# A sliding-window attention block with a gated MLP on one core: the split MLP weights are made once, kept in device memory and loaded as parts

## The chip, the core and the metric

The kernel runs on one core of a Trainium2 chip. The metric is the device time of one execution in microseconds. The kernel before took 1002.38 us as the median of three runs (999.41 to 1004.93).

The engines have these names here and in the profile: PE or TensorE (matrix products; PEld is its loading of weights), DVE or VectorE, ACT or ScalarE, POOL or GpSimd, and SP or SyncE, which in this kernel only issues transfers. Each of them works through its own instructions in program order.

## The reference, cut to what matters

```python
# x: 1 x 2048 x 640; wqkv 640 x 1920; wo 640 x 640; w1 640 x 1536; w2 1536 x 640
sa, ca, ga, sb, cb, gb = split6(silu(c) @ w_mod)          # each of 640
h = layernorm(x) * (1 + ca) + sa
q, k, v = heads(h @ wqkv)                                 # 32 heads of 20
p = softmax(mask(q @ k.T / sqrt(20)))                     # causal, window of 256
x = x + ga * (merge(p @ v) @ wo)
h = layernorm(x) * (1 + cb) + sb
y = layernorm(h)
x = x + gb * (gelu(y @ w1 + b1) @ w2 + b2)
```

All data is float32.

## The kernel before, in words

**Two parts for each operand.** Every large product is made from operands split into a high part (a copy rounded to the type `fp32r`) and a low part (the operand less its high part). Three products of parts, high by high, high by low and low by high, are added up. A split therefore costs a copy for the high part and a subtraction for the low part; the weights `w1` and `w2` are split like the activations.

**The attention** is a loop over steps `t`, some 3.7 us each from t = 12 (102 us) to t = 84 (380 us). A step makes scores for one block of 128 queries and four heads, takes their maximum, exponentiates transposed scores made eleven steps behind (LAG), and multiplies by v. Between these, each step does a number of products for q, k and v (`unit`), whose parts go through device memory (`q_scr`, `k_scr`) before they are loaded again for the scores (`rows_in`, 5 steps or so ahead). Everything else is hung on quarter steps by `spread(plan, steps, lo, hi)`: a list of closures under the key (t, quarter), run in that order. Tables of numbers at the top of the file (EXTRA, EARLY, AFTER, LNS, MODS, WOS, W1S, RS, TAIL_AT and more) say how many products a step takes and when each side task comes. MODS places the sums for three of the modulation vectors (`mod_steps`).

**The row blocks.** The 16 blocks of 128 rows go through the steps of `mid_steps`: load `ob`, scale (`om`), split (`oh`, `ol`), output product `wo`, add to x (`xb`), statistics, modulation and norm (`y`), transposes of x (`xt`) and y (`yt`), split of the transposed y (`yhi`, `ylo`). Four of them run during the last attention steps, the rest between the products of the MLP.

**The MLP** begins at about 576 us. It works through a written list, PLAN: a word is an operation (`ops`), a number says how many TensorE closures (`pe`) come next. Each TensorE closure is three products of 128 x 512. The rows stand in four chunks of 512, taken in pairs; p is the pair. For f = 0 to 5 the products P1 and P2 use a column block of w1 as it is; for i = 0 to 5 the products P3 to P7 use five sums and differences of the column blocks i and i + 6 of w1 (`w1_sums`, tile `cm`, tag `ws`), so that fewer products serve both chunks. `second(j, ms)` multiplies the gelu result j (0 to 47) by a row block of w2 and adds it to the five output sums.

**The weights in the MLP.** Each part is made again for each pair: `w1_load` (L855) and `w2_load` (L860) fetch a raw block of 320 KB on SP; `w1_high`, `w1_low`, `w1_sums`, `ws_high`, `ws_low`, `w2_high` and `w2_low` (L1607 to L1650) make the parts. High parts are copied on ACT; the engine of each low part and sum stands in a string, W1E, SUME, WSE or W2E (d DVE, p POOL). 36 raw blocks of w1 and 48 of w2 are loaded and split in all. GHE and GLE name the engines that split the gelu results (`ghi`, `glo`). The sixth modulation vector, the gate `gb`, is summed in the MLP too (tile `wm5`, words `gl`, `gs`, `gt`, `go`).

Two lines show the form of a split, here of w2:

```python
nc.scalar.copy(tl["w2", j][0], wt["w2", j])
engines[W2E[j]].tensor_tensor(lo, wt["w2", j], f32(hi), ALU.subtract)
```

All instructions carry the line L193, the helper that keeps them in program order, so the profile is read by tile names.

Of the kernel before, what the change touches and what calls it, by code (L numbers as in the profile page):

```python
# [9 lines left out]
F32 = mybir.dt.float32  # L10
# [31 lines left out]
UNITS = ((0, 'q1', 'k1', 'v0', 'v1', 'k2', 'q2', 'v2', 'q3', 'k3', 'v30', 'k40', 'q40', 'v40', 'q41', 'k41', 'v31', 'v41'), (1, 'k00', 'q10', 'q00', 'k10', 'q01', 'k01', 'k11', 'q11', 'v0', 'v1', 'k2', 'q2', 'q3', 'k3', 'v2', 'q4', 'v3', 'k4', 'v4'))  # L42
FAST = 10
LNS = [-9.75, -3.75, -1.0, -1.5, 0.75, -0.75, 0.0]
LOV = [1, 2, 3, 7, 8, 17, 18, 23, 24, 25, 35, 36, 37, 41, 43, 47, 52, 55, 57, 58]
HIA = [0, 4, 7]
# [10 lines left out]
EXTRA = {9: -2, 10: -3, 11: 5, 14: -4, 15: 3, 16: -4, 17: 2, 18: 1, 19: -3, 20: -4, 21: 6, 22: 1, 23: 1, 25: 4, 26: -3, 27: 3, 28: -3, 29: 7, 30: -5, 31: 1, 32: -3, 33: -1, 34: -1, 35: -3, 36: 3, 37: 9, 38: -8, 39: 3, 40: -3, 41: -8, 42: -2, 43: 3, 44: -3, 45: 9, 46: 3, 47: -1, 48: 4, 50: 1, 51: -3, 52: -16, 53: 7, 54: -5, 55: 4, 56: -7, 57: 13, 58: -1, 59: 10, 60: -1, 61: 3, 63: 2, 64: -1, 65: 10, 66: -4, 67: -1, 69: 2, 70: -4, 71: 4, 72: 3, 73: 3, 75: -9, 76: -2, 77: -3, 78: -1, 79: -1, 80: -4, 81: -9, 82: 15, 83: 6, 84: -2, 85: 2, 86: 2, 87: 11, 88: 4, 89: -9, 90: 3, 91: 1, 92: 3, 93: -6, 94: -12, 95: 1, 96: 1, 98: 3, 99: 2, 100: 2, 101: 7, 102: -3, 103: 6, 104: -4, 105: -1, 106: -6, 107: -2, 108: -1, 109: 7, 110: 1, 111: 3, 112: 4, 114: -1}  # L57

EARLY = {1: (4, 0, 0), 2: (5, 0, 0), 3: (5, 0, 0), 4: (2, 0, 0), 5: (3, 0, 0), 7: (3, 0, 0), 9: (5, 0, 0), 10: (5, 0, 0), 12: (1, 0, 0), 13: (0, 0, 0), 14: (0, 0, 0), 15: (5, 0, 0), 16: (5, 0, 0), 17: (4, 0, 0), 19: (4, 0, 0), 20: (2, 0, 0), 21: (4, 0, 0), 23: (5, 0, 0), 24: (1, 0, 0), 25: (1, 0, 0), 30: (5, 0, 0), 32: (0, 0, 0), 33: (3, 0, 0), 35: (5, 0, 0), 36: (1, 0, 0), 37: (5, 0, 0), 42: (1, 0, 0), 43: (2, 0, 0), 44: (5, 0, 0), 45: (5, 0, 0), 49: (4, 0, 0), 50: (3, 0, 0)}

AFTER = {0: 1, 2: 1, 4: 3, 5: 1, 6: 1, 7: 1, 8: 1, 9: 1, 10: 2, 11: 1, 12: 2, 14: 1, 15: 2, 19: 1, 20: 1, 21: 1, 22: 1, 23: 2, 25: 1, 27: 1, 32: 1, 34: 1, 35: 1, 36: 1, 38: 1, 39: 1, 40: 3, 41: 1, 43: 2}

SUMS_LAST = [14, 15, 18, 23, 25, 26, 27, 29, 35, 42, 50, 57, 59, 63, 64, 74, 76, 79, 83, 86, 88, 91, 92, 95, 101, 105, 106, 110, 116, 117, 118, 120, 121, 122, 123, 126, 129, 132, 133, 135, 136, 139]
LEAST = 4
CUT = 3
WHOLE = [11, 12, 23, 24, 26, 28, 29, 31, 38, 39, 40, 42, 43, 44, 45, 47, 50, 53, 55, 57, 60, 63, 75, 76, 84, 86, 90, 108, 109, 111, 112, 115, 116, 121, 122, 124, 125, 126, 127]
MOST = 10
MODS = [[8.75, 17.0], [18.75, 27.0], [70.25, 79.0]]
WOS = [89.25, 94.0, 99.0, 109.0, 111.75, 114.25, 115.75]
W1S = [118.25, 123.5, 135.0]  # L70
RS = [[79.5, 82.5], [86.0, 87.0]]
TOMID = 109
WARM = {(115, 0): 1, (121, 0): 3, (127, 2): 1, (130, 1): 2, (135, 0): 4, (136, 0): 10, (114, 3): 6, (120, 3): 1, (135, 2): 1}
LATE_AT = [105.75, 106.5, 106.75, 108.75, 110.25, 111, 113.25]
TAIL0 = [115.25, 120.25, 124.25, 129.25]
NEXT = [133.869, 138.565]
CROSS = [1.165, -0.035]
# [121 lines left out]
def block_kernel(ctx: ExitStack, tc: tile.TileContext, x, wqkv, wo, w1, b1, w2, b2, c, crow, wmod, wcol, sel, outT):  # L199
# [665 lines left out]
    def w1_steps():  # L865

        def load():
            w1_load(0)
            w1_load(1)
            w2_load(0)  # L870
# [942 lines left out]
```

## Time and profile before

| | |
|---|---|
| median of three runs | 1002.38 us |
| the profiled execution | 1001.14 us |
| its span, first to last instruction | 999.4 us |
| mean granted TensorE clock | 0.992 |
| attention, row blocks 0 to 4 or so | 0 to about 576 us |
| MLP and the other row blocks | about 576 to 999.4 us |
| moved by DMA | 160.05 MB, mean 160 GB/s |

A row of a stage gives the stretch, then each engine's busy time with its instructions in brackets, the granted share of the TensorE clock, the busy share of 16 DMA engines and the rate. A row of a group names engine, operation, output and inputs (with the buffer numbers left out), shapes, the count, busy time and mean length in ns, and after a bar the idle time of the engine before them with what ended it. A row of waits gives total time, times and the longest.

### The profile page before, as it was taken

The page shows a single profiled execution, that of the slowest core. Times are in us where ns is not written, and L with a number is a line of the kernel's source. Part 1 is how long each engine was busy: PE and PEld are TensorE (multiplying, and loading weights), DVE is VectorE, ACT ScalarE, POOL GpSimd, SP SyncE. Part 2 cuts the span into 40 slices and gives each one's busy share as a digit, 9 for nine tenths or more (in the row PEclk, how much of TensorE's full clock was granted, in tenths as well). Part 3 has the DMA queues.
Part 4 walks back from the last instruction along what each step waited for, and adds up shares of the span by engine and source line. Part 5 has one row for each costly group of instructions (what it writes and reads, how often), then busy time and mean ns, then how long its engine had stood idle before and what let it go on. Part 6 is the DMA issues. An engine that isn't in the chain of part 4 may idle for free.

```text
span 999.4 us, 20268 instructions
## 1 busy us (share of the span) xinstructions
PE 944.9 (95%) x7719; PEld 741.5 (74%) x7719; DVE 723.6 (72%) x1140; ACT 473.7 (47%) x830; POOL 534.0 (53%) x672
## 2 busy tenths in 40 slices
PE   9999999999999999999988988889999989989998
PEld 8777777777777777776776867768887777767876
DVE  6564877888767877777898688794658878766553
ACT  3724555656654555555545553543334435533232
POOL 3423555677873545645445566974334539952142
PEclk8999999999999999999999999999999999999999
DMA  8366778564787569566562274432227533421063
GB/s 302 105 216 189 244 239 269 170 206 148 232 244 192 165 189 279 160 168 190 148 170 75 78 240 129 131 102 72 79 67 235 169 111 117 125 83 53 27 186 104
DMA packets 102433, 160.05 MB, mean 160 GB/s; under 512 B 9248, under 2 KB 42496, under 8 KB 102336
## 3 DMA queue, kind: packets, MB, share of 16 engines
q1 hardware_dynamic: 93120, 150.37, 50.1%
q10 hardware_dynamic: 9216, 8.39, 2.7%
q8 instruction: 61, 1.00, 0.4%
q14 instruction: 36, 0.29, 0.1%
HBM read 106.38 MB, written 51.58 MB: 158 GB/s over the span
## 4 chain that ended last, share of the span: by engine, by line
PE 67%; DVE 18%; ACT 5%; issue 4%; DMA 3%; POOL 2%; SPq 0%; DVEq 0%; ACTq 0%; POOLq 0%
PE pp L193 16%; PE P L193 12%; PE out L193 9%; PE e L193 7%; PE o L193 7%; PE s L193 4%; PE wo L193 4%; ACT pt L193 3%; DVE e L193 3%; PE ppo L193 2%; DVE glo L193 2%; DVE nm L193 1%; DVE cm L193 1%; DMA ob<-o_scr 1%; DVE ghi L193 1%
## 5 line engine op out<-in xcount | busy, mean ns | idle before, releaser
L193 POOL TENSOR_SCALAR_AFFINE_SELECT pt<-pt 128x512 f32<-128x512 f32 x192 | 130.0, 677 | 138.6 <-ACT pt L193 131.5
L193 ACT ACTIVATE pt<-e 128x1024 f32<-128x1024 f32 (+1 forms) x120 | 133.7, 1114 | 65.3 <-DVE e L193 63.1
L193 DVE TENSOR_REDUCE nm<-s 128x1 f32<-128x256 f32 (+4 forms) x206 | 157.6, 797 | 4.4
L193 POOL TENSOR_TENSOR w2lo<-w2r,w2hi 128x640 fp32r<-128x640 f32 x46 | 81.4, 1770 | 96.3 <-ACT w2hi L193 85.7
L193 PE MATMUL e<-qbuf,kbuf 62*128 62x128 f32 (+2 forms) x773 | 111.8, 328 | 10.4 <-ACT pt L193 9.0
L193 PEld LDWEIGHTS e<-qbuf,kbuf 62*128 62x128 f32 x773 | 80.7, 185 | 49.5 <-ACT pt L193 25.6
L193 DVE COPY_PREDICATED e<-mask_t,e 128x512 f32<-128x512 uint32 x96 | 66.6, 694 | 68.8 <-PE e L193 62.5
L193 PE MATMUL pp<-hhi,w_hi 128*128 128x512 f32 x265 | 114.0, 430 | 0.2 <-ACT pf L193 0.2
L193 PE MATMUL s<-kbuf,qbuf 60*128 60x384 f32 (+2 forms) x728 | 105.9, 302 | 4.2 <-DVE nm L193 1.9
L193 PE MATMUL pp<-hlo,w_hi 128*128 128x512 f32 x265 | 108.4, 409 | 0.2 <-POOL hlo L193 0.2
L193 PE MATMUL pp<-hhi,w_lo 128*128 128x512 f32 x265 | 106.3, 401 | 0.0
L193 PE MATMUL out<-glo,w2hi 128*128 128x512 f32 x240 | 94.9, 395 | 7.2 <-DVE glo L193 7.0
L193 PEld LDWEIGHTS s<-kbuf,qbuf 60*128 60x128 f32 x728 | 89.2, 186 | 14.1 <-DVE nm L193 5.8
L193 PE MATMUL o<-pt,vbuf 128*32 128x128 f32 x2688 | 99.5, 277 | 0.0
L193 PE MATMUL out<-ghi,w2hi 128*128 128x512 f32 x240 | 96.5, 402 | 0.4 <-DVE xr L193 0.4
L193 PE MATMUL out<-ghi,w2lo 128*128 128x512 f32 x240 | 94.2, 392 | 0.1
L193 POOL TENSOR_TENSOR w_lo<-wraw,w_hi 128x128 fp32r<-128x128 f32 x171 | 76.0, 476 | 31.6 <-ACT w_hi L193 31.6
L193 ACT COPY oT<-o 128x128 f32<-128x128 f32 x128 | 33.9, 265 | 119.1 <-PE o L193 112.1
L193 DVE COPY_PREDICATED s<-mask_t,s 128x512 f32<-128x512 uint32 x112 | 77.1, 689 | 13.8 <-PE s L193 13.5
L193 PEld LDWEIGHTS o<-pt,vbuf 128*32 128x32 f32 x2688 | 66.9, 109 | 15.0 <-issue 2.7
L193 PEld LDWEIGHTS pp<-hhi,w_hi 128*128 128x128 f32 x265 | 49.9, 188 | 20.4 <-issue 11.3
L193 ACT ACTIVATE gs<-gs,b_sb 128x512 f32<-128x512 f32 x24 | 17.4, 723 | 89.3 <-DVE gs L193 89.3
(445 smaller groups left out, 2155.8 us busy)
## 6 DMA issues: line engine op xcount, KB each, us to landing
w2r<-in_w SPq DMA_DIRECT2D x48, 320.0 KB
qbuf<-q_scr SPq DMA_DIRECT2D x60, 240.0 KB
wraw<-in_wqkv SPq DMA_DIRECT2D x36, 320.0 KB
w1r<-in_w SPq DMA_DIRECT2D x36, 320.0 KB
kbuf<-k_scr SPq DMA_DIRECT2D x44, 240.0 KB
q_scr<-stage SPq DMA_DIRECT2D x20, 512.0 KB
k_scr<-stage SPq DMA_DIRECT2D x20, 512.0 KB
o_scr<-oT ACTq DMA_DIRECT2D x64, 128.0 KB
```

Of the source, the lines that this page charges most:

```text
L193: return self.tc.keep_in_program_order(op(*args, **kw))
```

## The change: weights split once and kept

- The parts of w1 (column blocks 0 to 5), of w2 (twelve row blocks) and of the sums of blocks (six times twelve blocks of 128 x 128) are made once, by `prepare()`, between about t = 8 and t = 86 of the attention, and stored in three new buffers of device memory, `w1_scr`, `w2_scr` and `ws_scr`. A piece is a copy on ACT, a subtraction on the engine in PREPE (31 times POOL, 5 times DVE) a quarter step later, and a store on SP some steps later (PREPS). There are 36 pieces: 18 of 640 columns, and for each of the six sums three of 384, 640 and 512 columns. The five additions of a sum run on the engines in the new SUME (25 times POOL, 5 times DVE). A raw block is loaded AHEAD = 4 steps before its piece.
- In the MLP, `w1_take`, `ws_take` and `w2_take` load both parts in one transfer, of 640 KB, or 1.5 MB for a sum. The words that loaded raw weights and made parts leave PLAN; w2 has three buffers (W2B) instead of two for the parts and two for the raw blocks.
- The first blocks are loaded as parts in the attention, without a copy or subtraction there.
- The gate `gb` is summed during the attention (t = 59 to 68.75, `mod_steps(5, None)`, `column`).
- A dictionary MOVE says for each word of PLAN that splits or copies which engine does it, in place of the strings. It has 25 low halves of the gelu results on DVE and 23 on POOL (GLE: 44 and 4), and of the high halves 19 on DVE, 12 on POOL and 17 on ACT (GHE: 33, 2 and 13). The two additions of `raw` become two words.
- The order of blocks inside a sum's tile changes, and with it the indices in `product`; the number of products doesn't.
- EXTRA, EARLY, AFTER, LNS, LOV, HIA, SUMS_LAST, WHOLE, MODS, WOS, W1S, RS, WARM, LATE_AT, TAIL_AT, UNITS and PLAN get new numbers and order.

```diff
+PREPS = [1.5, 2.0, 1.5, 1.5, 1.5, 1.5, 1.5, 1.5, 0.75, 1.25, 1.5, 1.25, 1.0, 1.75, 1.5, 1.75, 1.5, 1.5, 1.5, 1.5, 2.0, 1.5, 1.5, 2.0, 1.75, 2.5, 0.5, 1.5, 1.0, 1.5, 1.75, 1.5, 1.5, 1.5, 1.75, 1.5]
+PREPE = 'ppppppppdpppppdppppdppppppppddpppppp'
+SUME = 'ppppppppppppddpppddppppppppppd'
+AHEAD = 4.0
+W2B = 3
...
+    w2_scr = scratch("w2_scr", [FT, P, 2, D])
+    w1_scr = scratch("w1_scr", [HF, P, 2, D])
+    ws_scr = scratch("ws_scr", [HF, P, 2, 12 * P])
...
+        def column():
+            ps = aside([P, KT], "pmc")
+            for j in range(KT):
+                matmul(ps[:, j : j + 1], box["acc"][:, j * P : (j + 1) * P], ones[:, 0:1], start=True, stop=True)
+            nc.vector.tensor_copy(gb, ps)
+            nc.vector.tensor_tensor(gb2, gb, b2_sb, ALU.mult)
...
-    def w1_load(k):
...
-    def w2_load(i):
...
+    def kept(dst, src):
+        nc.sync.dma_start(f32(dst).rearrange("p z k m -> p z (k m)") if len(dst.shape) == 4 else f32(dst), src)
+
+    def prepare():
+
+        box = wop.tile([P, 2, KT - 1, D], F32R, tag="wo", name="prep").rearrange("p a k n -> p (a k) n")
+        raws, parts = [], []
...
+        def load(src, at):
+            n = len(raws)
+            raws.append([f32(box[:, n % 4]), 0])
+            at = max([at] + [r[1] + 0.25 for r in raws[-5:-4]])
+            later(at, lambda: nc.sync.dma_start(raws[n][0], src))
+            return raws[n]
+
+        def piece(raw, k, c, scr, to):
+            n = len(parts)
+            at, hold, e = PREP[n], PREPS[n], engines[PREPE[n]]
+            parts.append(at + hold + 0.25)
+            hi, lo = [box[:, 4 + 2 * (n % 2) + z, 0 : c * P] for z in range(2)]
+            src = raw[0][:, k * P : (k + c) * P]
+            later(at, lambda: nc.scalar.copy(hi, src))
+            later(at + 0.25, lambda: e.tensor_tensor(lo, src, f32(hi), ALU.subtract))
+
+            def store():
+                nc.sync.dma_start(scr[:, :, to * P : (to + c) * P], f32(box[:, 4 + 2 * (n % 2) : 6 + 2 * (n % 2), 0 : c * P]))
+
+            later(at + hold, store)
+            raw[1] = at + 0.25
+
+        for name in PREPO:
+            kind, i = name[0], int(name[1:])
+            at = PREP[len(parts)] - AHEAD
+            if kind != "s":
+                src, scr = (w1, w1_scr) if kind == "a" else (w2, w2_scr)
+                piece(load(src[i], at), 0, KT, scr[i], 0)
+                continue
+            ra, rb = load(w1[i], at), load(w1[i + HF], at)
...
+            piece(rb, 2, 3, ws_scr[i], 9)
...
+            piece(rb, 0, 5, ws_scr[i], 0)
+            piece(ra, 0, 4, ws_scr[i], 5)
...
+    def eng(default):
+        return engines[MOVE.get(word_[0], default)]
...
-    def w2_high(j):
-        tl["w2", j] = [mp.tile([P, D], F32R, tag=f"w2{n}", bufs=2, name=f"w2{n}{j}") for n in ("hi", "lo")]
-        nc.scalar.copy(tl["w2", j][0], wt["w2", j])
-
-    def w2_low(j):
-        hi, lo = tl["w2", j]
-        engines[W2E[j]].tensor_tensor(lo, wt["w2", j], f32(hi), ALU.subtract)
...
+    def ws_take(p, i):
+        t = w1_tile(f"w1s{p}{i}")
+        tl["ws", p, i] = [t[:, 0], t[:, 1]]
+        kept(t, ws_scr[i])
+
+    def w2_take(j):
+        t = mp.tile([P, 2, D], F32R, tag="w2", bufs=W2B, name=f"w2{j}")
+        tl["w2", j] = [t[:, 0], t[:, 1]]
+        kept(t, w2_scr[w2_order[j]])
...
-    def g_low(j):
-        hi, lo = tl["g", j]
-        engines[GLE[j]].tensor_tensor(lo, tl["gr", j], f32(hi), ALU.subtract)
...
+        eng(GLE[j]).tensor_tensor(lo, tl["gr", j], f32(hi), ALU.subtract)
```

More of the change, by code (lines that the diff above doesn't have):

```diff
@@ L157 @@
+cl33 st32 cl34 st33 st34
 """
@@ L850, in wo_steps @@
         return [step(1, lambda f=f, kt=kt: f(*kt)) for f, *kt in steps]
-    w1_order = (list(range(HF)) + [f + HF * z for f in range(HF) for z in range(2)]) * 2
+    engines = {"d": nc.vector, "p": nc.gpsimd, "a": nc.scalar}
     w2_order = (list(range(FT)) + [f + HF * z for f in range(HF) for z in range(2)]) * 2
-    def w1_load(k):
-        if k < len(w1_order):
-            wt["w1", k] = lw.tile([P, KT, P], F32, tag="wraw", bufs=2, name=f"w1r{k}")
-            nc.sync.dma_start(wt["w1", k].rearrange("p k m -> p (k m)"), w1[w1_order[k]])
@@ L860, in w2_load @@
-    def w2_load(i):
-        if i < len(w2_order):
-            wt["w2", i] = box2["mid"].tile([P, D], F32, tag="raw2", bufs=2, name=f"w2r{i}")
-            nc.sync.dma_start(wt["w2", i], w2[w2_order[i]])
-    def w1_steps():
[L867 to L870, printed above, removed]
-        def high():
-            wt["w1"] = w_tiles("w10")
-            nc.scalar.copy(wt["w1"][0], wt["w1", 0])
-        def low():
-            nc.vector.tensor_tensor(wt["w1"][1], wt["w1", 0], f32(wt["w1"][0]), ALU.subtract)
-        return [step(1, go) for go in (load, high, low)]
+    def kept(dst, src):
+        nc.sync.dma_start(f32(dst).rearrange("p z k m -> p z (k m)") if len(dst.shape) == 4 else f32(dst), src)
@@ new lines, in w1_steps, with first, second @@
+    def w1_steps():
+        def first():
+            wt["w1"] = [w_tiles("w10"), [lw.tile([P, KT, P], F32R, tag="wraw", bufs=2, name=f"w11{n}") for n in ("hi", "lo")]]
+            for f in range(2):
+                for z in range(2):
+                    nc.sync.dma_start(f32(wt["w1"][f][z]).rearrange("p k m -> p (k m)"), w1_scr[f, :, z])
+        def second():
+            t = box2["mid"].tile([P, 2, D], F32R, tag="raw2", name="w20")
+            kept(t, w2_scr[0])
+            wt["w2"] = [t[:, 0], t[:, 1]]
+        return [step(1, go) for go in (first, second)]
@@ L1071, in mid_steps @@
         if ch % 2:
-            steps.update({nm: [combine(nm)] for nm in COMB if SPAN[bg]})
+            steps.update({nm: [combine(nm, z) for z in range(1 + (nm == "raw"))] for nm in COMB if SPAN[bg]})
             times = dict(times)
@@ L1763, in block_kernel @@
         if word in ops:
+            word_[0] = word
             ops.pop(word)()
```

314 lines of the change are left out of this document (139 added, 175 removed).

## The prediction

> **What bounds the kernel now.** I read the page first, then the busy time by stage, who waits for whom, and the chain of work that ended last.
>
> ```profile
> span 999.4 us, 20268 instructions
> PE 944.9 (95%) x7719; PEld 741.5 (74%) x7719; DVE 723.6 (72%) x1140; ACT 473.7 (47%) x830; POOL 534.0 (53%) x672
> ```
>
> TensorE is the busiest engine at 95%, so what can be won is its 54.5 us of idle time and whatever runs below speed. The stages say where that is. The columns are the stretch, its length, then busy time and instructions of PE, PEld, DVE, ACT and POOL, the granted clock, the DMA share and GB/s. First the stretch of the attention where the change puts its new work, and the MLP:
>
> ```profile
> 102.00:384.00 282.00, 277.68 (x3060) 205.82 (x3060) 222.92 (x327) 157.14 (x295) 171.29 (x277) 1.00 0.71 209
> 576.00:999.40 423.40, 390.04 (x1877) 317.72 (x1865) 296.52 (x446) 168.19 (x269) 223.79 (x187) 0.99 0.39 119
> ```
>
> In the first TensorE idles 282.00 - 277.68 = 4.3 us, in the second 423.40 - 390.04 = 33.4 us. So the MLP, not the attention, has time to give. Within the MLP:
>
> ```profile
> 576.00:660.00 84.00, 69.98 (x397) 56.90 (x385) 72.69 (x111) 44.49 (x75) 64.37 (x54) 0.98 0.54 165
> 660.00:740.00 80.00, 79.40 (x374) 66.80 (x375) 47.02 (x74) 23.09 (x32) 34.54 (x32) 1.00 0.25 74
> 740.00:860.00 120.00, 112.61 (x560) 90.95 (x560) 97.41 (x158) 55.94 (x98) 70.08 (x67) 1.00 0.50 152
> 860.00:950.00 90.00, 83.83 (x359) 67.70 (x358) 56.90 (x80) 30.25 (x43) 36.33 (x25) 0.98 0.20 58
> 950.00:999.40 49.40, 44.22 (x192) 35.38 (x190) 22.50 (x27) 14.43 (x22) 18.48 (x12) 0.98 0.47 147
> ```
>
> The idle times are 14.0, 0.6, 7.4, 6.2 and 5.2 us. The stage from 660 to 740 shows what the same products do when nothing is late. The others hold either the row blocks' second half (output product, norm, transposes) or a VectorE instruction that takes too long. The waits of TensorE in the MLP say the same (us in total, times, longest):
>
> ```profile
> PE out L193 <- DVE glo L193: 7.0, 4, 2.2
> PE yt L193 <- ACT y L193: 5.8, 6, 2.4
> PE yt L193 <- DVE ylo L193: 5.3, 6, 1.7
> PE wo L193 <- DVE xb L193: 5.1, 3, 3.3
> ```
>
> Three of the four are steps of row blocks on loaded in-order queues. The largest is the low half of a gelu result. The chain around one of its waits, and the two engines' instructions at that moment:
>
> ```profile
> 883.46 3.45 PE P L193 x15
> ...
> 894.13 3.03 DVE glo L193
> ...
> 897.94 5.01 PE P L193 x15
> ```
> ```profile
> 893.85 2.75 POOL L193 TENSOR_TENSOR w1s13lo<-cm,w1s13hi 128x1152 fp32r<-128x1152 f32 x1
> ```
> ```profile
> L193 DVE TENSOR_TENSOR glo<-gr,ghi x21: 629/692/3017, 590.4 to 948.4; 128x512 fp32r<-128x512 f32 x21
> ```
>
> This `glo` has a median of 692 ns, yet here it takes 3.03 us: it starts 0.28 us after GpSimd's 2.75 us split of a weight sum and ends 0.56 us after it, a normal length less a little. It was held back by the GpSimd instruction. The 15 products after the wait then need 5.01 us where the same 15 needed 3.45 before: 1.6 us more at a lower clock (0.98 in three of the stages above; 0.02 of their 223.4 us is 4.5 us).
>
> **What leaves the MLP.** The same stages once more, for the instructions of one tile alone: first all that read the raw second weights, then all that read the raw first weights (busy time of DVE, ACT, POOL in both), then those of the sixth modulation vector, which the change moves into the attention (PE, PEld, DVE):
>
> ```profile
> 576.00:660.00 84.00, 0.00 (x0) 5.05 (x7) 13.37 (x7) 0.98 0.54 165
> 740.00:860.00 120.00, 0.00 (x0) 12.46 (x18) 29.85 (x17) 1.00 0.50 152
> sum 423.40, DVE 1.65 ACT 34.72 POOL 81.39; mean DVE 0.33 ACT 6.94 POOL 16.28
> ```
> ```profile
> 576.00:660.00 84.00, 14.14 (x14) 4.66 (x7) 3.72 (x3) 0.98 0.54 165
> 740.00:860.00 120.00, 9.60 (x8) 3.28 (x5) 3.19 (x2) 1.00 0.50 152
> sum 423.40, DVE 34.27 ACT 13.91 POOL 33.00; mean DVE 6.85 ACT 2.78 POOL 6.60
> ```
> ```profile
> 576.00:660.00 84.00, 1.17 (x10) 1.27 (x10) 7.44 (x5) 0.98 0.54 165
> ```
> ```profile
> L193 ACT CAST w1s00hi<-cm x1: 1154/1154/1154, 637.0 to 637.0; 128x1152 fp32r<-128x1152 f32 x1
> L193 POOL TENSOR_TENSOR w1s00lo<-cm,w1s00hi x1: 2667/2667/2667, 642.5 to 642.5; 128x1152 fp32r<-128x1152 f32 x1
> ```
>
> The splits of the twelve block sums come on top, 12 x 1.154 = 13.8 us on ACT and twelve of about 2.7 us, nine on POOL (24) and three on DVE (8 at this price). Together the MLP loses some 34 + 8 + 7 + 2 = 51 us on DVE of 296.5, 62 on ACT of 168.2 and 138 on POOL of 223.8. The new table MOVE then takes gelu splits off VectorE: it names 25 low halves for DVE where GLE has 44, and 19 high halves where GHE has 33.
>
> Per stage, I let TensorE's idle time shrink as the ratio of busy to free time of VectorE does, which is my assumption. 576 to 660: DVE 72.69 - 14.14 - 7.44 = 51.1 of 84, its ratio falls from 6.43 to 1.55, so 14.0 falls to 3.4: **-10.6**. 740 to 860: 97.41 - 9.60 is 87.8; a quarter of the moved gelu splits (19 x 0.69 plus 14 of about the same, 23 us) makes it 82 of 120, ratio 4.31 to 2.17: 7.4 falls to 3.7, **-3.7**. 860 to 950: the GpSimd splits that held `glo` back are gone, **-5.5** of 6.2. After 950: 5.2 holds the last stores, **-1**. The clock gives back **-3.5** of 4.5. Gaps too short to show as idle time I put at **-2**. Sum: **-26**. If everything went but 4 of the last stage's 5.2, it would be 33.4 + 4.5 - 4 = 34; the other end is a loss, since the added loads could be late (below).
>
> On the held `glo` a rule bears, and it also speaks against this change. The Trainium skill, page "SBUF — State Buffer", section "Who interferes with whom", says that a VectorE instruction with two SBUF inputs and a GpSimd instruction that reads SBUF share a port, which the first holds for its whole length. The trace agrees (3.03 us against 692 ns). But by that rule the 23 low halves that MOVE puts on POOL can hold up those left on VectorE just as the weight splits did; then 860 to 950 would give about 3 in place of 5.5, and the sum below would be 980.5.
>
> **What the MLP loads instead.** Before, 36 + 48 loads of 320 KB (27.5 MB); after, 47 of 640 KB, ten of 640 KB and twelve of 1.5 MB, about 56 MB. The MLP's 119 GB/s become 119 + 28.7 MB / 423 us = 187. On SP each load of block sums waits until TensorE has left the buffer two loads back; queued behind it are the next w2 parts and row-block loads, and the products of the next block wait for it. The cover is one block, 54 products at 3.45 / 15 = 0.23 us, 12.4 us; 1.5 MB at the rate below (399 GB/s) needs 4. I take nothing; if the cover failed by half a transfer each time, 12 x 2 = +24.
>
> **What comes into the attention (about 102 to 384 us).** 36 pieces with 18 x 640 + 6 x 1,536 = 20,736 columns in all, 25 block sums on POOL and 5 on DVE, five loads and products of the modulation vector, 30 weight loads, 36 stores. The prices:
>
> ```profile
> L193 ACT CAST w_hi<-wraw 128x640 fp32r<-128x640 f32 x36 | 26.2, 728 | 7.1 <-DMA wraw<-in_wqkv 6.9
> L193 POOL TENSOR_TENSOR ot_lo<-ob,ot_hi 128x640 fp32r<-128x640 f32 x7 | 10.9, 1557 | 8.2 <-ACT ot_hi L193 8.2
> L193 DVE TENSOR_TENSOR ot_lo<-ob,ot_hi 128x640 fp32r<-128x640 f32 x9 | 8.8, 973 | 0.8 <-ACT ot_hi L193 0.8
> ```
> ```profile
> L193 POOL TENSOR_TENSOR cm<-w1r x4: 734/736/799, 660.8 to 863.3; 128x256 f32<-128x256 f32 x4
> ```
> ```profile
> PE s L193 <- DVE nm L193: 1.9, 3, 0.9
> PE e L193 <- ACT pt L193: 1.7, 5, 0.6
> ```
> ```profile
> SPq L193 <- POOL stage L193: 56.1, 18, 8.1
> ```
>
> ACT: 20,736 / 640 x 0.728 = 23.6 us, 157 to 181 of 282. POOL: 31 of the pieces (all but 3,072 columns, so 17,664), 43.0 us, and 25 x 0.736 = 18.4: 171 to 233 of 282 (83%). DVE: ten at most 0.97 and five modulation products of about that: +14, to 237 (84%). The PE rows are TensorE's two longest waits from 100 to 384 us, 3.6 us together. All three engines stay under the span, so this is a cost of lateness, not of sums. The ratio of busy to free grows from 1.26 to 1.8 on ACT and 3.8 to 5.3 on DVE: +1.5 us of these waits. POOL's goes from 1.5 to 4.8, but TensorE waited for POOL hardly at all here; +1. SP is in order: each store waits for its low half on POOL, and behind it stand the next q and k rows and wqkv loads; it waits so already (the SPq row, from 100 to 400 us), and TensorE does not feel it. With the modulation loads there are 71 more issues; for these and the transfers, +0.5. The bounds are 0 (it all lies in free time) and +29 (the rival below). The retuned tables (EXTRA, EARLY, AFTER, LOV and the like) only shift work by slots, and seven fewer warming products go: 0, within 3 either way. Sum for the attention: **+3**.
>
> Sum: -26 + 3 = -23. The profiled execution took 1001.14 us (span 999.4), so 978. It is 1.2 below the median of 1002.38, inside the runs' 999.41 to 1004.93, so I make no correction. A measurement here can tell about 0.5% (5 us).
>
> **Rivals.** *The transfers of the attention become the bound (slower).* The rows:
>
> ```profile
> 7.00:17.00 10.00, 9.34 (x70) 9.18 (x70) 7.63 (x25) 3.77 (x5) 5.28 (x10) 0.86 1.04 399
> ```
> ```profile
> 250.00:300.00 50.00, 49.55 (x557) 36.70 (x556) 35.45 (x50) 28.65 (x50) 39.03 (x61) 1.00 0.82 239
> ```
> ```profile
> w2r<-in_w SPq DMA_DIRECT2D x48, 320.0 KB
> w1r<-in_w SPq DMA_DIRECT2D x36, 320.0 KB
> ```
>
> Added are 35 loads of 320 KB (11.5 MB) and 20,736 x 2 x 128 x 4 B = 21.2 MB of stores: 32.7 MB. From 102 to 384 the engines carry 209 GB/s at a share of 0.71, or 294 at full share; at that rate 32.7 MB need 111 us and only 0.29 x 282 = 82 are free: +29 us of late q and k rows, and after each wait 1.6 us of lower clock, some +6. Time 1001 - 26 + 3 + 35 = 1013. It decides when the added traffic gets less than 32.7 MB / 82 us = 399 GB/s, just what the stretch from 7 to 17 us sustained. Against it: at a share of 0.82 (250 to 300) TensorE is busy 49.55 of 50 us, and a packet's time includes its waiting, so 0.71 overstates what is used. Chance 0.12. The Trainium skill's page "DMA: Bandwidth & Descriptors", section "Specifications", puts one core's HBM limit at about 358 GB/s; the row of 399 contradicts it, and the measurement decides; by the page this rival would have a higher chance.
>
> *POOL, at 83%, becomes late in the attention.* With the busy-to-free ratio tripled, TensorE's 3.6 us of waits triple too (+7), and late low halves of q, k and the weights I put at 4 more: +11 in place of +3, 986. Chance 0.13.
>
> *The MLP's waits are the length of a row block's chain, not load.* `y`, `ylo` and `xb` are serial steps; if they stay, only `glo`, the last stage and half the clock go, -8: 1001 - 8 + 3 = 996, no change within 0.5%. Against it: 660 to 740 has a light DVE and no wait. Chance 0.10.
>
> **The numbers.** Forecast 978, chance 0.63 (own range 966 to 988); the rest, 0.02, is late loads in the MLP, which I count as no change. Low 962: all 34 of the MLP and the attention at its lower bound, with a little for the tables (1001 - 34 - 3 = 964, less 2). High 997: both rivals of the middle lie inside, the DMA rival (0.12) outside. Faster by over 0.5%: 0.63 + 0.13 + a third of 0.10 = 0.79. Same: 0.09. Slower: 0.12.
>
> **What would show it.** In the changed profile: the MLP stretch about 26 us shorter, with no wait for `glo` over 1 us, POOL's busy time in it down by 100 or more, TensorE's waits for `y`, `ylo` and `xb` below half. The stretch of the attention: POOL about 83% busy, DMA share near 1, TensorE still at 98%, at most 5 us longer. The prediction is wrong if the scores wait for q or k rows, if the attention is over 12 us longer, or if the MLP keeps its waits with an idle VectorE.

## The result

The changed kernel took 992.88 us, the median of five runs (990.73 to 994.52), against 1004.09 for the kernel before (five runs, 999.41 to 1004.93): ratio 0.9896, 95% interval 0.9867 to 0.9926. Run again later on another chip it took 991.64, ratio 0.99 (0.9848 to 0.9951). It is 1% faster; 978 had been forecast, so the gain is less than half of what was expected. The profiled execution took 994.52 us, the slowest of its five. Its page, and the same stages as before:

```profile
span 992.8 us, 20133 instructions
PE 947.6 (95%) x7705; PEld 748.9 (75%) x7705; DVE 645.3 (65%) x1081; ACT 424.8 (43%) x752; POOL 491.5 (50%) x673
```
```profile
102.00:403.00 301.00, 287.35 (x3082) 211.74 (x3084) 236.31 (x336) 181.13 (x336) 234.21 (x331) 0.98 0.92 303
595.00:992.80 397.80, 384.94 (x1904) 321.28 (x1904) 208.94 (x387) 98.42 (x154) 119.44 (x138) 0.99 0.58 199
```

To part the change into its two halves I use one instruction that both kernels have: VectorE's mask of the 128th and last block of scores. Its row in the time line of the changed kernel, and in that of the kernel before:

```profile
555.53 0.68 DVE L190 COPY_PREDICATED s<-mask_t,s 128x512 f32<-128x512 uint32 x1
```
```profile
536.45 0.68 DVE L193 COPY_PREDICATED s<-mask_t,s 128x512 f32<-128x512 uint32 x1
```

It starts 19.1 us later, and the rest of the span (992.8 - 555.5 = 437.3 against 999.4 - 536.4 = 463.0) is 25.7 us shorter. The MLP gave what was forecast (26). The attention cost 19 where 3 were forecast. I follow this step's start, "the last score step", through all experiments. It moves from one execution to another: the changed kernel has it at 555.5 and, run again, at 553.6, and two kernels below that differ from it in the MLP alone have it at 552.7 and 560.0. So a single execution tells a difference in the attention only beyond some 7 us. Whole times spread too: the nine runs of the changed kernel lie between 988.36 and 1000.75 us.

**The MLP after.** The stages that answer to the five of before, then TensorE's waits and the low halves of the gelu results:

```profile
595.00:679.00 84.00, 78.38 (x464) 66.98 (x465) 58.65 (x118) 27.86 (x47) 46.66 (x53) 0.96 0.64 212
679.00:760.00 81.00, 81.00 (x383) 68.22 (x382) 34.22 (x56) 15.09 (x21) 9.29 (x11) 1.00 0.42 156
760.00:870.00 110.00, 108.16 (x546) 89.66 (x545) 74.98 (x153) 35.22 (x57) 50.10 (x62) 1.00 0.72 236
870.00:950.00 80.00, 80.00 (x355) 66.24 (x354) 31.76 (x49) 14.90 (x21) 6.65 (x7) 1.00 0.45 165
950.00:992.80 42.80, 37.39 (x164) 30.18 (x162) 9.33 (x15) 5.34 (x8) 6.75 (x7) 1.00 0.62 219
```
```profile
PE wo L190 <- DVE xb L190: 3.0, 1, 3.0
PE out L190 <- DMA w<-w_scr: 1.4, 1, 1.4
...
PE out L190 <- POOL glo L190: 1.0, 1, 1.0
...
PE yt L190 <- DVE ylo L190: 0.4, 1, 0.4
...
PE yt L190 <- ACT y L190: 0.2, 1, 0.2
```
```profile
L190 DVE TENSOR_TENSOR glo<-gr,ghi x13: 676/692/869, 616.2 to 941.5; 128x512 fp32r<-128x512 f32 x13
```

TensorE's idle time by stage is now 5.6, 0, 1.8, 0 and 5.4 us where it was 14.0, 0.6, 7.4, 6.2 and 5.2. The waits for `y` and `ylo` are gone but for 0.6 us, that for `xb` fell from 5.1 to 3.0, and VectorE's longest `glo` takes 869 ns where one took 3017.

**The attention after.** TensorE's waits from 102 to 403 us, and three stretches of 50 us:

```profile
PE s L190 <- DMA kbuf<-k_scr: 3.7, 4, 2.0
PE e L190 <- ACT pt L190: 3.3, 6, 1.1
PE pmr L190 <- ACT oT L190: 1.9, 1, 1.9
PE e L190 <- DMA qbuf<-mlo: 1.9, 1, 1.9
```
```profile
100.00:150.00 50.00, 49.76 (x509) 36.60 (x508) 40.66 (x55) 29.75 (x60) 40.99 (x55) 1.00 0.99 326
150.00:200.00 50.00, 46.87 (x484) 34.24 (x484) 39.54 (x62) 28.49 (x52) 36.83 (x56) 0.93 0.92 309
...
250.00:300.00 50.00, 49.57 (x552) 36.95 (x552) 35.30 (x49) 32.66 (x58) 45.51 (x61) 1.00 0.98 321
```

Waits for transfers, of which before had none worth a row, now lead: rows of k (`kbuf`) and the low row of the maxima (`mlo`, 16 KB, made every eighth step and needed two to three steps later). TensorE idles 301.00 - 287.35 = 13.7 us here against 4.3, and the clock of 0.98 costs some 5 to 6 more (0.02 x 301). The loss is not even: two of these stretches run at a share of 0.98 and 0.99 and lose nothing; it falls at single steps. One of them, in TensorE's time line:

```profile
177.61 0.38 PE L190 MATMUL s<-kbuf,qbuf 60*128 60x128 f32 x1 [1.97 <-DMA kbuf<-k_scr]
```

That step (31) takes 6.9 us in place of 3.4, and the next, which waits for nothing, 5.8 in place of 4.0, at a granted clock of 0.62.

### The profile page after: what moved, and what is told of

It is laid out like the page before. It is cut to its first block, busy times and chain, and to the rows that moved or that the text cites. A ratio compares the mean times of both kernels' runs of the same rounds, so it can differ in the third digit from the quotient of the medians.

```text
span 992.8 us, 20133 instructions
## 1 busy us (share of the span) xinstructions
PE 947.6 (95%) x7705; PEld 748.9 (75%) x7705; DVE 645.3 (65%) x1081; ACT 424.8 (43%) x752; POOL 491.5 (50%) x673
## 5 line engine op out<-in xcount | busy, mean ns | idle before, releaser
L190 PE MATMUL out<-ghi,w 128*128 128x512 f32 x480 | 172.9, 399 | 1.5 <-DMA w<-w_scr 1.4
L190 DVE TENSOR_REDUCE nm<-s 128x3 f32<-128x768 f32 (+4 forms) x200 | 157.2, 816 | 4.4
L190 PE MATMUL e<-qbuf,kbuf 62*128 62x128 f32 (+2 forms) x773 | 114.4, 332 | 15.0 <-ACT pt L190 10.1
L190 PE MATMUL s<-kbuf,qbuf 60*128 60x256 f32 (+2 forms) x728 | 108.1, 305 | 7.5 <-DMA kbuf<-k_scr 3.7
L190 PEld LDWEIGHTS out<-ghi,w 128*128 128x128 f32 x480 | 90.8, 189 | 18.8 <-DVE glo L190 1.8
L190 PE MATMUL o<-pt,vbuf 128*32 128x128 f32 x2688 | 102.0, 282 | 0.0
L190 PE MATMUL out<-glo,w 128*128 128x512 f32 x240 | 94.4, 394 | 1.0 <-POOL glo L190 1.0
L190 PE MATMUL P<-yhi,w1s 128*128 128x512 f32 x264 | 88.5, 389 | 0.0
L190 POOL TENSOR_TENSOR w_lo<-wraw,w_hi 128x128 fp32r<-128x128 f32 (+1 forms) x166 | 75.6, 486 | 20.9 <-ACT w_hi L190 20.9
L190 POOL TENSOR_TENSOR prep<-prep 128x256 f32<-128x256 f32 (+4 forms) x56 | 61.2, 1098 | 22.3 <-ACT prep L190 21.3
```

Source lines behind the costliest of these rows:

```text
L190: return self.tc.keep_in_program_order(op(*args, **kw))
```

## The experiments

My theory was that the transfers cost the 19 us. The rivals were the engines' added work (POOL and VectorE at 78%), and the order of SP's queue, in which a store that waits holds up the rows behind it. Where no number of runs is given a kernel was run once.

**The engines' work without the transfers.**

```diff
-            later(at, lambda: nc.sync.dma_start(raws[n][0], src))
+            if n < 4:
+                later(at, lambda: nc.sync.dma_start(raws[n][0], src))
...
-            later(at + hold, store)
+            if n < 3:
+                later(at + hold, store)
...
-        kept(t, w2_scr[w2_order[j]])
+        kept(t, w1_scr[j % 3])
```

> The changed kernel without the transfers of the preparation in the attention: all copies, subtractions and sums stay on their engines, but only the first four raw blocks are loaded and only the first three pieces stored, and the MLP loads its parts from those three pieces again and again (same bytes, other values, so weights and output are not the reference's). The last score step of the attention stands at 536.4 us in the kernel before and 555.5 in the changed one. Theory 'transfers' (the 16 DMA engines are full from 102 to 403 us and the rows of q, k and the maxima come late, with the clock drop that follows a wait): it falls back to 536 to 541, the DMA share of that stretch to about 0.6 to 0.7, the whole to about 975. Rival 'engines' (POOL, ACT and DVE are late because of the added copies, subtractions and sums): it stays at 551 to 557 and the whole at 989 to 994.

Measured: 976.74 us, the last score step at 541.3, 4.9 later than before. Its attention:

```profile
102.00:400.00 298.00, 291.29 (x3198) 215.19 (x3197) 242.12 (x344) 185.04 (x346) 239.36 (x341) 1.00 0.73 224
```

POOL is as busy as in the changed kernel (239 of 298 us), yet TensorE idles only 6.7 us. So the engines' work, together with the new tables, costs about 5 of the 19 us.

**The transfers without the engines' work.**

```diff
-            later(at, lambda: nc.scalar.copy(hi, src))
-            later(at + 0.25, lambda: e.tensor_tensor(lo, src, f32(hi), ALU.subtract))
+            if n < 2:
+                later(at, lambda: nc.scalar.copy(hi, src))
+                later(at + 0.25, lambda: e.tensor_tensor(lo, src, f32(hi), ALU.subtract))
...
-                later(at, lambda dst=dst, x=x, y=y, op=op, e=engines[SUME[5 * i + n]]: e.tensor_tensor(dst, x, y, op))
```

> The changed kernel with all transfers of the preparation but without its work on the engines: only the first two pieces are copied and subtracted, the other 34 pieces store the same buffers again, and no sums are made (so the weights of the MLP and the output are not the reference's). Theory 'transfers': the last score step stays at 549 to 557 us with a DMA share over 0.88 in the stretch from 102 us on, waits of the scores for q, k or maxima rows remain. Rival 'engines': it falls to 536 to 542. If both have a share it lies between, and the two runs' parts need not add up.

Measured: 991.16 us, the last score step at 553.7 (+17.3).

```profile
102.00:400.00 298.00, 285.96 (x3070) 210.90 (x3068) 225.13 (x325) 160.79 (x300) 174.37 (x276) 0.98 0.92 304
```

POOL and ACT are back at the load of before (174 and 161 us), and nearly all of the loss is still there, within what one execution can tell. The first kernel's 541.3 is over 11 us below the lowest of the four executions named above. The transfers are the cause.

**Bytes or order.** The same transfers at the same places in the queue, but a quarter of the bytes:

```diff
-            later(at, lambda: nc.sync.dma_start(raws[n][0], src))
+            pp = P if n < 4 else P // 4
+            later(at, lambda: nc.sync.dma_start(raws[n][0][0:pp], src[0:pp]))
...
-                nc.sync.dma_start(scr[:, :, to * P : (to + c) * P], f32(box[...]))
+                pp = P if n < 3 else P // 4
+                nc.sync.dma_start(scr[0:pp, :, to * P : (to + c) * P], f32(box[0:pp, ...]))
...
```

> All transfers of the preparation are still issued at their places and waited for, but from the fifth load and the fourth store on they move only 32 of the 128 partitions, a quarter of the bytes (some 8 MB of 30 are left); the engines' work is unchanged. The later pieces are so not computed from the weights, and the MLP loads the first three stored pieces again in the same sizes, so only the time is read. If the cost of the attention is the rate (bytes), the 128th score step starts near where it does without the transfers: 4 to 8 us later than before (540 to 544 us), the whole at 977 to 981. If it is the order on SyncE's queue (each store waits for its low half and the next rows stand behind it), that is all still there: 14 to 19 us later (550 to 556) and 988 to 994.

Measured: 978.89 us, the last score step at 543.1 (+6.7).

```profile
102.00:400.00 298.00, 290.14 (x3180) 214.25 (x3182) 241.56 (x344) 185.59 (x345) 238.99 (x339) 1.00 0.80 245
```

With every issue and every wait in place, 12.4 of the 19.1 us are gone. So the bytes (and the packets that carry them) set the cost; the number of issues does not. At 245 GB/s and a share of 0.80 the attention hardly suffers, at 302 and 0.92 it does.

**Two ways around SP's queue.** First the 36 stores on ScalarE's queue:

```diff
-                nc.sync.dma_start(scr[:, :, to * P : (to + c) * P], ...)
+                nc.scalar.dma_start(scr[:, :, to * P : (to + c) * P], ...)
```

> The changed kernel with the 36 stores of the preparation issued on ACT's queue in place of SP's; the bytes are the same. Theory 'transfers' in the form 'rows stand in SP's queue behind long stores': the rows overtake, the last score step falls by 6 to 14 us from 555.5. In the form 'the engines are simply full': it stays within 4 us. Rival 'engines': the same or later, since ACT has to wait for the low halves from POOL and issue 36 transfers (0.33 us each, 12 us).

Measured: 1002.63, the last score step at 566.0. Then the rows of q, k and the maxima on ScalarE's queue in place of the stores:

```diff
-            nc.sync.dma_start(f32(to[64 * e : 64 * e + 60, :, c0 ...
+            nc.scalar.dma_start(f32(to[64 * e : 64 * e + 60, :, c0 ...
...
```

> The changed kernel with the loads of q and k rows and of the maxima rows issued on ACT's queue in place of SP's (the second maxima row a quarter step later). Theory 'transfers' in the form 'rows stand in SP's queue behind the preparation': TensorE's waits for k rows and maxima rows (7.5 us in the changed kernel up to 418 us) go, and the clock drops after them, the last score step falls by 6 to 14 us. In the form 'engines are full': within 4 us. Rival 'engines': later, since ACT waits for TensorE to leave the buffers and issues some 130 more transfers.

Measured: 1028.09, the last score step at 589.6. Neither came out as the theory of the transfers had it; the rival's forecast was later, since ScalarE has to wait, and later they are. Of the second kernel, TensorE's waits and the row of the attention:

```profile
PE e L190 <- ACT pt L190: 14.5, 10, 4.4
PE psx L190 <- ACT oT L190: 5.5, 2, 3.1
PE pp L190 <- ACT pf L190: 4.8, 3, 1.8
```
```profile
102.00:400.00 298.00, 263.06 (x2741) 192.92 (x2745) 212.06 (x304) 160.82 (x304) 209.96 (x299) 0.95 0.85 280
```

ScalarE also works in order: an issue that has to wait holds up the exponentials (`pt`) behind it, and TensorE waits for those. In the first kernel this is seen only in part: from 102 to 400 us TensorE waits 4.6 us for other results of ScalarE (`vbuf`, `hf`), but 4.8 for the low row. The Trainium skill, page "DMA: Bandwidth & Descriptors", section "Issuing engines are not separate DMA queues", says that transfers run on the same DMA engines whichever engine issues them, and that several issuers save only issuing time. Nothing here speaks against it: 280 GB/s at a share of 0.85, no more than the 303 of one queue, though this kernel also waits more.

**The maxima rows alone on ScalarE's queue.** Twice, since in the first form the low row went out up to 5.3 us after it was ready:

```diff
-            nc.sync.dma_start(f32(qb_[(half * QUADS + quad) % NSLOT][row::64]), f32(part))
+            go = lambda row=row, part=part: nc.scalar.dma_start(f32(qb_[(half * QUADS + quad) % NSLOT][row::64]), f32(part))
+            if row == 60:
+                go()
+            else:
+                put(now[0] + 1, 3, go)
```

> As the changed kernel, but the two 16 KB rows of maxima of each group of heads are issued on ScalarE's queue (the high row behind its own copy, the low one a step later) instead of behind the preparation's loads and stores on SyncE's. If late maxima rows and the lower clock behind them are a main part of the loss, no wait for the low row is left and the 128th score step starts 4 to 7 us earlier than the changed kernel's 555.5, the whole at 986 to 991. If the rate alone is what counts, the products then wait for the rows of k instead and the step stays within 2 us of 555.5.

Measured: 1010.9, with 15.0 us of waits for that row (8 times), the last score step at 575.2. The second form, `put(now[0] + 1, 1, go)`:

> The maxima rows on ScalarE's queue again, the low row now issued where GpSimd ends it in place of half a step later. If the late issue was the cause of 1010.9, the waits for the low row (15.0 us) fall below 5 and the time is 988 to 995. If ScalarE's queue itself is the cause (a waiting issue holds up its exponentials), it stays above 1000.

Measured: 989.76, four runs from 986.78 to 995.62, ratio 0.9874 (0.9835 to 0.9913); the profiled run, at 995.62 the slowest, has its last score step at 559.2 and these waits:

```profile
PE e L190 <- DMA qbuf<-mlo: 7.4, 6, 1.8
PE e L190 <- ACT pt L190: 7.1, 13, 1.1
```

So the late issue had been the first form's trouble, and the time is as expected of that theory; the waits did not fall below 5 us as expected. (The row still went out up to 5.1 us after it was ready; the median fell from 2.3 to 1.3 us. On SP's queue it is 0.03 us, at worst 4.7.) In its six waits this 16 KB row came 3.6 to 6.0 us after its issue, and in the kernel with a quarter of the bytes 4.5 to 5.6 in three: a queue of its own does not make a small row quick. Over its nine issues from 100 to 400 us it landed 3.9 us after the issue in the median, in the changed kernel, on SP's queue, 2.0. What is left to choose is how early it is issued.

**Rows of q and k asked for earlier** (`READ = 7` to `8`):

> As the changed kernel, but the rows of q and k are asked for up to one score step (3.7 us) earlier where a buffer is free. If their lateness is a short queue ahead of them (order), the waits for rows of k (3.7 us) go and the 128th score step is 3 to 5 us earlier than 555.5. If the queue is full for long (rate), asking earlier gains nothing: within 2 us.

Measured: 1000.1, the last score step at 566.3. Not better, against both theories: TensorE still waited 3.9 us for rows of k and 3.7 for the low row, and the granted clock from 102 to 400 us was 0.95. By its time this one execution lies at the end of the changed kernel's own runs, by its last score step 6 us beyond the four executions; whether it is worse is not shown, and why it should be I did not settle.

**The preparation spread** over steps 5 to 106 of 128, four runs:

```diff
+PREP = [5.25 + round(1.38 * 4 * (t - 12.25)) / 4 for t in PREP]
...
```

> The changed kernel with the preparation spread over more of the attention: every time in PREP is 5.25 + 1.38 x (t - 12.25), so it runs from about t = 5 to t = 106 in place of 12 to 86 (the buffer is needed by the output weights only from t = 108.5). Bytes and instructions are the same. Transfers as the cause: the added traffic falls from 103 to some 80 GB/s, the DMA share of 102 to 400 us from 0.92 to about 0.86, the last score step from 555.5 to 545 to 551 us and the whole by 5 to 10. If only the number of transfers on SP mattered and not their rate, it stays within 3 us.

Measured: 990.49 (988.25 to 995.81), ratio 0.987 (0.9836 to 0.9905), the last score step at 553.3: no clear difference from the changed kernel. The forecast of the transfers' rate (545 to 551) failed, and what the rival had said came true (within 3 us). The rate fell to 282 GB/s and the clock stayed at 1.00, but 16.8 us of loss stayed. So the mean rate of the stretch alone does not set the cost: at 282 GB/s and a share of 0.88 as much is lost as at 302 and 0.92. With the raw blocks shared, so that six loads go, the median was higher, not 1 to 3 us lower as forecast:

```diff
+PREPO = [f'{k}{n}' for i in range(HF) for k, n in (('a', i), ('s', i), ('b', 2 * i), ('b', 2 * i + 1))]
...
+                if kind == "a":
+                    ra = raws_a
...
```

> As the spread kernel, and six of the 30 raw loads left out: the order of the preparation is a block of w1, the sum that uses the same block, two blocks of w2, so the sum takes the raw block that is there already (2 of 32 MB less, and three blocks less at once in the queue). Transfers as the cause: another 1 to 3 us less than the spread kernel. If the rate had nothing to do with it: the same as the changed kernel.

Measured: 996.01, ratio 0.9927 (0.9902 to 0.9953). Up to step 88 it was 10.1 us behind the kernel before, and then lost 14 more by step 104, 5.1 of them in one wait for the low row of the maxima. A spread with the first form of the maxima rows on ScalarE's queue:

> The preparation spread from step 5 to 106 of 128 in place of 12 to 84, and the rows of maxima on ScalarE's queue. In the kernel with the spread alone TensorE waited 5.2 us for the low row of maxima and 1.7 for rows of k. If the rows' place in the queue behind large transfers is what is left, the 128th score step starts at 543 to 549 us and the time is 981 to 987. If only the bytes count, it stays at 551 to 555 and 988 to 992.

Measured: 1008.03, ratio 1.0039 (1.0012 to 1.0066), the last score step at 571.5 against a forecast of 543 to 549. By what the two forms showed, its late row spoils it.

**One place in the queue.** The long waits at step 90 have a place. SP's time line there in the changed kernel:

```profile
403.52 0.34 SPq L190 DMA_DIRECT2D ga_b<-row_scr  x1
404.57 5.00 SPq L190 DMA_DIRECT2D wor<-in_wo  x4
409.67 0.90 SPq L190 DMA_DIRECT2D q_scr<-stage  x2
410.66 1.00 SPq L190 DMA_DIRECT2D qbuf<-mhi  x1
411.76 1.08 SPq L190 DMA_DIRECT2D qbuf<-mlo  x1
```

The low row is ready at 407.0 and goes out at 411.8, behind four loads of the output weights that the changed tables ask for at step 87 (`WOS[0]`), where before it was 89.25. Those four issues take 5.00 us; in the kernel with a quarter of the bytes they take 2.13, in the kernel before 1.85. The issues themselves are short; the rest of the 5.00 us SP waits between them:

```profile
L190 SPq DMA_DIRECT2D wor<-in_wo x4: 327/342/423, 404.6 to 409.2; - x4
```

What it waits for is in the semaphore records of the traces. In both kernels all transfers of SP and ScalarE share eight semaphores, and an issue waits until the transfer that had its semaphore before has landed; never are more than eight on the way. The fourth load goes out at 409.24, 0.02 us after the landing of a store of `o_scr` that ScalarE had issued at 402.45 with the same semaphore. From 100 to 403 us SP was held like this for 83.7 us (76 times) in the changed kernel, for 16.8 (12 times) in the kernel before from 100 to 384; from 100 to 400 for 59.1 with a quarter of the bytes, for 30.5 without the transfers, for 54.7 with the preparation spread. With the rows on ScalarE's queue ScalarE was held for 40.8. Of the waits that the profile lists for SP in the first two stretches the largest of this kind are:

```profile
SPq L190 <- DMA o_scr<-oT: 39.9, 17, 4.4
```
```profile
SPq L193 <- DMA o_scr<-oT: 10.4, 4, 6.8
```

So nearly half of this is spent behind stores of attention results that are not the preparation's; they land later on the fuller engines (median 5.6 us after their issue, before 3.4). No run has more semaphores, so what this limit costs is not shown. The four loads put back:

```diff
-WOS = [87.0, 94.25, 99.0, 108.5, 111.75, 113.75, 117.75]
+WOS = [89.25, 94.25, 99.0, 108.5, 111.75, 113.75, 117.75]
```

> As the changed kernel, but the first loads of the output weights and of their factor row are asked for at step 89.25, as in the kernel before, in place of step 87, so that the maxima rows of step 88 are issued ahead of them. If the wait at step 90 (1.70 us, and 2.7 us in steps 90 and 91 together) is that place in the queue, it goes, and the 128th score step starts 2 to 3 us earlier than 555.5; the time is 988 to 991. If the rate alone counts, another transfer is late in its place and the time stays at 991 to 994.

Measured in four runs: 988.19 (986.76 to 989.69), ratio 0.9849 (0.9828 to 0.987). The wait at step 90 is gone: from step 88 to 96 this kernel gains 0.2 us on the kernel before, where the changed one lost 2.6. Its last score step stands at 554.1 all the same, not 2 to 3 us earlier as forecast, since steps 66 and 67, which come before the edit, lost 5.8 us in this execution and 3.6 and 2.1 in the changed kernel's two. The same in the spread kernel:

> The same in the kernel whose preparation is spread from step 5 to 106, where steps 90 and 91 lost 5.8 us. If the queue's order is the cause, the wait of 3.6 us goes, the 128th score step starts at 547 to 550 in place of 553.3 and the time is 984 to 987, below both kernels. If the rate counts, 989 to 992.

Measured: 987.88 (986.82 to 988.44), ratio 0.9847 (0.9827 to 0.9868), the last score step at 551.6; a little short of what I expected, and no faster than the other. Both have the lowest medians here. Against the changed kernel (0.9896 and 0.99) the intervals touch; what is shown is the 2.8 us at the place itself (6.0 in the spread kernel, from step 88 to 96).

**The same at step 64.** The 5.8 us of steps 66 and 67 come by a late store of k that SP waits for. A store and a load of the preparation moved out of its way, and the changed kernel itself run beside it:

```diff
+PREPS[23], PREP[26] = 3.5, 68.25
```

> The kernel that asks for the output weights at step 89.25, and also with the preparation's store of step 62.75 put to 64.25 and one of its loads from step 63.25 to 64.25, so that the store of k ahead of the rows of step 64 finds a shorter queue. In the kernel before this edit SyncE waits 4.5 us there for that store to land, the maxima rows go out 2 us after they are ready, and steps 66 and 67 lose 5.8 us. If the place in the queue is the cause, the loss of steps 63 to 67 falls from 8 to below 4 us, the 128th score step starts at 549 to 552 and the time is 983 to 987. If the rate counts, the loss appears at another step: 553 to 555 and 987 to 990.

> The changed kernel itself, beside the next two on one chip. If its loss in the attention belongs to the kernel, its 128th score step starts at 553 to 557 again and the time is 990 to 995; if it belongs to the chip, both differ by over 4 us.

Measured: 991.64 for the changed kernel, its last score step at 553.6, as expected; 996.62 for the edit (989.15 to 998.14), ratio 0.9924 (0.9895 to 0.9954), its last score step at 559.6, so it failed. The wait for the low row at step 66 did go. In its place stands one of 6.5 us for ScalarE, whose time line says why:

```profile
319.93 0.72 ACT L191 CAST prep<-prep 128x640 fp32r<-128x640 f32 x1 [7.43 <-DMA ws_scr<-prep]
320.56 0.58 ACT L191 COPY vT<-pp 128x512 f32<-128x512 f32 x1
```

The store that I put later releases the buffer for a later high part. That copy now waits 7.43 us on ScalarE, and behind it stands `vT`, for which TensorE waits. The changed kernel has shorter waits of this kind, five of them, which I had not foreseen:

```profile
ACT prep L190 <- DMA w_scr<-prep: 13.4, 5, 4.7
```

**The MLP's two parts.** MOVE emptied, so that the gelu splits go back to the engines of before:

```diff
+MOVE = {}
```

> The changed kernel with an empty table MOVE, so that the splits of gelu results and row blocks go to the engines that the old strings name: 44 low halves of gelu results on DVE, 4 on POOL. The weights stay prepared. My account of the MLP (VectorE's busy share sets TensorE's waits): DVE's busy time in the MLP rises from 209 by about 20 to 30 us and the MLP gets 4 to 8 us longer (half or less of the 26 us that it lost came from MOVE). Rival (the GpSimd splits that held VectorE back were all of it): the MLP stays within 2 us. Second rival (the engine table is what gave the gain, not the weights): the MLP gets 15 us or more longer.

And the changed kernel with 47 idle subtractions of 512 columns on GpSimd, one with each load of w2:

```diff
+        d = mp.tile([P, CHUNK], F32, tag="dummy", name=f"dummy{j}")
+        nc.gpsimd.tensor_tensor(d, box2["cb"][:, 0:CHUNK], box2["sb"][:, 0:CHUNK], ALU.subtract)
```

> The changed kernel with one needless GpSimd subtraction of 512 columns, two SBUF inputs, issued with each of the 47 loads of w2 parts (about 1.29 us each, 60 us in all; the result is not used). Nothing waits for them but GpSimd's own later instructions and whatever needs the port. If GpSimd splits held VectorE back: low halves of gelu results on DVE again take up to 2 us (at most 0.87 in the changed kernel), and the MLP gets 4 to 10 us longer. If only VectorE's own work counted: the MLP stays within 2 us.

From the first product P to the end the changed kernel takes 392.7 us (before 420.8; in thirteen other executions with the same work in the MLP 387.5 to 391.0, so this one was on the long side). Without MOVE it is 397.4 (the whole 996.55), with the idle subtractions 398.9 (the whole 1003.9, its last score step at 560.0): 5 and 6 us by this execution, 6 to 11 by the others. Without MOVE the MLP is still 23.4 us shorter than before, so the weights, not the engine table, give most of the gain. The forecast's reason for the 4 to 8 us did not hold: VectorE's busy time in the MLP rose by 9 us, not by 20 to 30. The low halves on VectorE with the idle subtractions:

```profile
L190 DVE TENSOR_TENSOR glo<-gr,ghi x13: 678/694/1347, 619.6 to 950.7; 128x512 fp32r<-128x512 f32 x13
...
L190 DVE TENSOR_TENSOR glo<-gs,ghi x12: 678/692/1769, 769.9 to 988.6; 128x512 fp32r<-128x512 f32 x12
```

GpSimd work that no one needs makes VectorE's longest low half 1769 ns, and the MLP longer. VectorE, with the same instructions, is busy for 225 us from the first product P on in place of 207. TensorE's waits for GpSimd's own low halves grew only from 1.0 to 1.5 us. So splits on GpSimd cost time by holding up VectorE; how much of the 6 us came from GpSimd's own later results in the row blocks, and what splits cost by their own length, was not measured apart.

## Why the prediction was right in the MLP and wrong in the attention

**The MLP, -26 forecast, -25.7 measured.** By stages, idle time fell by 8.4 (10.6 forecast), 5.6 (3.7), 6.2 (5.5) and, in the last, not at all (1): 20 us against 20.8. The 5 to 6 us left of the 25.7 answer to the clock (3.5) and the short gaps (2), but the clock of the whole stretch stayed at 0.99 in this execution, so that split of the rest is not shown. That the two numbers agree to 0.3 us is partly luck: in the second execution of the changed kernel the MLP's clock was 1.00 and the rest of the span 29.9 us shorter than before, and over the thirteen others the gain is 26.3 to 32.1. So the forecast lies at the low end of what was measured. That idle time shrinks as VectorE's ratio of busy to free time stays an assumption that fitted. POOL's busy time fell from 223.8 to 119.4 us, by 104 as the "100 or more" said. The larger loads came in time but for one wait of 1.4 us.

On the held `glo` the measured change is the one to look at: the stage that had 6.2 us of idle time has none, though GpSimd makes 23 low halves of 1.29 us in the MLP. The rule of the Trainium skill's page "SBUF — State Buffer", section "Who interferes with whom", which by the prediction would have left 3 of the 5.5 us gained, agrees with the mechanism (the idle subtractions show it again, at 1769 ns) but not with that size: VectorE's longest `glo` is 869 ns. The traces' start and end times say why. Before, 30 of VectorE's 44 low halves ran beside a GpSimd instruction; now 3 of 25 do, all beside short ones (at most 1.07 us). The low halves that GpSimd makes hardly ever meet those of VectorE, so the rule was not put to the test by them.

**The attention, +3 forecast, +19.1 measured.** The step that failed is "with the modulation loads there are 71 more issues; for these and the transfers, +0.5". The transfers cost 12 to 14 us (19.1 less the 6.7 with a quarter of the bytes, or less the 4.9 without them; by the spread of the last score step between executions, 10 to 19). The other terms, +1.5 for ACT and VectorE and +1 for POOL, stand against 4.9 measured without the transfers. The loads on the engines were right: ACT 181 us, as forecast, and POOL 234 for 233.

The mechanism had been written down as the first rival, with a chance of 0.12 and 1013 us. Its rate was near: it took 294 GB/s as what the engines carry at full share, and the stretch then ran at 303. (That 91.6 MB, 58.9 of before and 32.7 added, need 302 us at 303 and the stretch lasted 301 says only that the bytes were counted rightly.) Its price was not: with its +29 and +6 the attention would have cost 38, which is as far above the 19.1 as the forecast's 3 is below. What was wrong was to price its mechanism at next to nothing in the sum, on two arguments. The first was a stretch at a share of 0.82 (250 to 300 us) in which TensorE was busy 49.55 us. The changed kernel shows that same stretch at a share of 0.98 and still at 49.57: it has no row that comes late, full or not, and so said nothing about steps 31, 63, 66 and 90, which have. The second was that a share of 0.71 overstates what is used. It does, but by 326 GB/s against 294, not by the 399 that were needed; the row of 399 lasted 10 us. At 326 the 91.6 MB take 281 us, all of the 282. The Trainium skill's page "DMA: Bandwidth & Descriptors", section "Specifications", puts a core's HBM limit at about 358 GB/s, and the prediction set the row of 399 against it. That row stands, but only for 10 us; the best of the 50 us stretches, 326, agrees with the page. By the prediction's own test its figure would have spoken for the rival (358 x 82 us are 29 MB, an estimate, and 32.7 were added), though the 82 us of that test rest on the 294.

Of the signs that the prediction named, DMA share near 1 held (0.92), TensorE at 98% did not (95%), and two of its signs of error came true: scores wait for rows of k, and the attention is over 12 us longer. In the MLP the wait for `xb` did not fall below half (3.0 of 5.1 us; 1.8 in the second execution). The rival of a late POOL falls, with POOL at 78% and TensorE idle for 6.7 us without the transfers. So does that of a chain in the MLP for `y` and `ylo`, which wait no more; `xb` keeps part of its wait.

What stays open: how much of the transfers' 12 to 14 us is the rate of the DMA engines and how much the eight transfers that may be on the way at once, which no run parts; why spreading the transfers won nothing; why asking for rows earlier did not help; and how much a better order could win. One place was worth 2.8 us; at a second the wait only changed its engine.

## What to carry over

When work is moved from a stage with idle engines to one that looks free, add up its bytes as carefully as its instructions, and divide by a rate that the traced kernel has held for as long as that stage lasts, not by its best 10 us. A calm stretch at a high DMA share proves nothing for other stretches: look for the small rows that are needed soonest after they are made, see what is queued ahead of them and how many transfers may be on the way at once, and ask what each would wait. A transfer put on a computing engine's queue, or a buffer that is released by a store, makes that engine wait in order, and its other readers with it.

## What had not been expected of the hardware

- SP's time goes into waits between issues more than into issues: the four loads of the output weights took SP 5.00 us at this place, against 1.85 in the kernel before, but each issue only 0.33 to 0.42, against 0.43. The low row's issue itself did take 1.08 us against 0.55.
- Where TensorE waited for the 16 KB row, it went on 3.4 to 7.6 us after the row's issue, in every kernel with such a wait, on SP's queue and on ScalarE's. Those are the late ones: in the stretches named above the row landed 2.0 us after its issue in the median, at most 4.6 (in the kernel before 1.9 and 2.7).
- Three waits of TensorE of 1.7 to 2.0 us were each followed by a step at a granted clock of 0.62 to 0.78 in the attention too, which adds 1.2 to 1.8 us to a step that waits for nothing. Not each time: a wait of 1.95 us at step 81 left the clock at 1.00, and so did that of 1.96 us at step 66 in the second run of the changed kernel.
